# One weight row of wo split into sixteen uneven transfers, four one-row stores, and the small input loads on SyncE's queue

## The chip, the cores and the metric

The kernel runs on one core of one Trainium2 chip. The metric is device microseconds of one execution; the median of the three runs shown for the kernel before is 353.46 us (353.4, 353.46 and 354.35). One more execution was profiled; its own time was 353.3 us.

## The reference

A gated mix of two decode blocks for a single token. Cut to what matters:

```python
g = sigmoid((x * gate_w).sum(-1))            # one scalar
q = (x @ wq)                                  # 32 heads of 128
scores = q . k_cache * 128 ** -0.5            # 8 KV heads, 32768 keys, 4 q heads to each
o = softmax(scores) @ v_cache
a = o.reshape(1, 32 * 128) @ wo               # wo: 4096 x 512
b = (silu(x @ w_gate) * (x @ w_up)) @ w_down  # 512 -> 1792 -> 512
out = g * a + (1 - g) * b                     # 512 values, bf16
```

Everything is bf16. The K and V caches have 8 x 32768 x 128 values each, so nearly all that is read from memory is cache; wq and wo have 4 MB each, the three matrices of the second block 1.8 MB each.

## The kernel before, in words

The work is written as one instruction list for each engine, with semaphores between them; nothing is scheduled by a planner, so the order in the code is the order on the engine.

**SyncE (SP) issues all the large loads**, on one queue, in this order: wq (L297), w_gate and w_up (L299), then the K and V caches (L280). Each of the 8 groups (one KV head) has two K blocks and two V blocks of 4 MB. Four pages of on-chip memory hold them, so a load waits until the page's last reader is done: a K page until PE has transposed its last piece (`sem_fill`), a V page until PE has multiplied it (`sem_v_free`). Ahead of the last V block, SP issues the first piece of wo (`load_wo(0)`, L316); behind that V block come w_down (L322) and the other four pieces of wo. wo stands in memory as 128 partitions by 32 rows of 512 values; `WO_CUTS = [0, 8, 18, 26, 30, 32]` cuts the 32 rows into five pieces, each with a semaphore of its own (`sem_wo`).

**TensorE (PE)** first turns x and gate_w into columns (L338), multiplies with wq (L351), w_gate and w_up (L375), and then loops over the groups: transposes of K (L390), scores (L402), and the product with V (L446) of the group before. `emit_end` (L479) is the end of the program: the sum of the exponentials (L481), the last reduction (L428), w_down (L458), then the pieces of wo. Rows 0 to 17 (pieces 0 and 1) go through `emit_wide` (L458, one matmul for each row), rows 18 to 31 through `emit_rows` (L469, four matmuls for each row, one for each quarter of the output). Before each piece PE waits for that piece's semaphore (L501). After piece 2 the wide part is added (L513).

**VectorE (DVE)** copies transposed K to on-chip memory (L671) and at the end writes the result, `res_row` (L713): the four quarters of 128 values lie on partitions 0, 32, 64 and 96.

**ScalarE (ACT)** starts with two small loads, x and gate_w, one row of 512 values each (L527, L528), on its own queue. It computes the exponentials (L548). At the end SP stores the first two quarters of the result and ACT the other two (`store`, L204), each in one transfer of two rows. SP then waits for both (`sem_out` at 32, L329), and the program ends with the barrier of all engines (L210).

**GpSimd (POOL)** makes constants and takes the maximum over the partitions (L273); after the last of these, at about 319 us, it has nothing left but the closing barrier.

Of the kernel before, what the change touches and what calls it, by code (L numbers as in the profile page):

```python
# [13 lines left out]
def bass_gated_mix__gqa_block_cached__swiglu_ffn__decode_kernel(  # L14
# [41 lines left out]
    SCALE = float(DH) ** -0.5  # L56
    assert UPG == STEP == 4 * HPG and UPP % NKT == 0 and UPP % NST == 0
    assert KC * H * DH <= PAGE and 2 * KC * F <= PAGE and WOJ * NOUT <= PAGE
    WO_CUTS = [0, 8, 18, 26, 30, 32]
    WIDE = WO_CUTS[2]  # L60
    OC = NOUT // 128

    RQ = 4
# [10 lines left out]
    with ExitStack() as es:  # L74
        def S_(name):
            return es.enter_context(nc.semaphore(name))
# [3 lines left out]
        sem_f = S_("s_f")  # L80
        sem_wo = [S_(f"s_wo{i}") for i in range(len(WO_CUTS) - 1)]
        sem_ld_x = S_("s_ld_x")
# [5 lines left out]
        sem_out = S_("s_out")  # L88
# [39 lines left out]
        def T(name, shape, dt):  # L128
            return es.enter_context(nc.sbuf_tensor(name, shape, dt))

        x_row = T("x_row", [1, D], BF16)
        gw_row = T("gw_row", [1, D], BF16)
# [43 lines left out]
        res_row = T("res_row", [128, 128], BF16)  # L176
# [25 lines left out]
        wo_v = page[:, PG_X, 0 : WOJ * NOUT].rearrange("p (j n) -> p j n", j=WOJ)  # L202

        def store(eng, k):  # L204
            eng.dma_start(
                out[0, 0, 256 * k : 256 * (k + 1)].rearrange("(c n) -> c n", c=2),
                res_row[64 * k : 64 * k + 33 : 32, :],
            ).then_inc(sem_out, 16)

        with nc.Block("main") as block:  # L210
            @block.gpsimd
            def _(pool):
                pool.memset(ones_bf[:, :], 1.0).then_inc(sem_const, 1)
                pool.memset(ones_f[:, :], 1.0).then_inc(sem_const, 1)
                npool = [0]

                def chain(ins):
                    ins.then_inc(sem_pool, 1)
                    npool[0] += 1
                    pool.wait_ge(sem_pool, npool[0])  # L220

                chain(pool.memset(ident[:, :], 0.0))
                pool.affine_select(
                    out=ident[:, :],
                    in_=ident[:, :],
                    compare_op=ALU.not_equal,
                    fill=1.0,
                    base=0,
                    pattern=[[-1, 128]],
                    channel_multiplier=1,  # L230
                ).then_inc(sem_ident, 1)
                chain(pool.memset(ident_f[:, :], 0.0))
                pool.affine_select(
                    out=ident_f[:, :],
                    in_=ident_f[:, :],
                    compare_op=ALU.not_equal,
                    fill=1.0,
                    base=0,
                    pattern=[[-1, 128]],
                    channel_multiplier=1,  # L240
                ).then_inc(sem_ident, 1)
                chain(pool.memset(perm[:, :, :], 0.0))
                for e in range(2):
                    pool.affine_select(
                        out=perm[:, e, :],
                        in_=perm[:, e, :],
                        compare_op=ALU.not_equal,
                        fill=1.0,
                        base=-e,
                        pattern=[[0, 2], [-2, 64]],  # L250
                        channel_multiplier=1,
                    ).then_inc(sem_ident, 1)
                pool.iota(
                    colidx[:, :],
                    pattern=[[1, 128]],
                    base=0,
                    channel_multiplier=0,
                    allow_small_or_imprecise_dtypes=True,
                ).then_inc(sem_iota, 1)
                pool.iota(  # L260
                    kf[:, :],
                    pattern=[[1, 1]],
                    base=0,
                    channel_multiplier=1,
                    allow_small_or_imprecise_dtypes=True,
                ).then_inc(sem_iota, 1)
                pool.wait_ge(sem_dve_gpart, 1)
                pool.partition_all_reduce(gtot[:, :], gpart[:, :], 128, ReduceOp.add).then_inc(
                    sem_gtot, 1
                )  # L270
                for g in range(G):
                    pool.wait_ge(sem_pmax, STEP * (g + 1))
                    pool.partition_all_reduce(  # L273
                        gmax[:, g, :], pmax[:, g * STEP : g * STEP + HPG], 128, ReduceOp.max
                    ).then_inc(sem_gmax, 1)

            @block.sync
            def _(sp):
                def cache(which, g, b, p, sem):
                    sp.dma_start(  # L280
                        page[:, p, :].rearrange("p (r d) -> p r d", d=DH),
                        which[0, g, b * BLK : (b + 1) * BLK, :].rearrange("(p r) d -> p r d", r=R),
                    ).then_inc(sem, 16)

                def load_k(g, b):
                    if g:
                        sp.wait_ge(sem_fill, UPG * (g - 1) + UPP * (b + 1))
                    cache(A_k_cache, g, b, PG_K[b], sem_page[PG_K[b]])

                def load_v(g, b):  # L290
                    if g:
                        sp.wait_ge(sem_v_free, NB * (g - 1) + b + 1)
                    elif PG_V[b] == PG_F:
                        sp.wait_ge(sem_pe_h, 1)
                    cache(A_v_cache, g, b, PG_V[b], sem_page[PG_V[b]])

                sp.dma_start(wq_v, A_wq.rearrange("(p c) n -> p c n", c=KC)).then_inc(sem_q, 16)  # L297
                for w, src in enumerate((B_w_gate, B_w_up)):
                    sp.dma_start(  # L299
                        wgu[:, w, :, :], src.rearrange("(p c) f -> p c f", c=KC)  # L300
                    ).then_inc(sem_f, 16)
                for b in range(NB):
                    load_k(0, b)
                load_v(0, 0)
                load_k(1, 0)
                load_v(0, 1)
                load_k(1, 1)
                for g in range(2, G):
                    for b in range(NB):
                        load_k(g, b)  # L310
                        load_v(g - 1, b)

                def load_wo(k):
                    a, b = WO_CUTS[k], WO_CUTS[k + 1]
                    src = A_wo.rearrange("(p j) n -> p j n", j=WOJ)
                    sp.dma_start(wo_v[:, a:b, :], src[:, a:b, :]).then_inc(sem_wo[k], 16)  # L316

                load_v(G - 1, 0)
                sp.wait_ge(sem_pe_q, 1)
                load_wo(0)  # L320
                load_v(G - 1, 1)
                sp.dma_start(  # L322
                    wd[:, :, :], B_w_down.rearrange("(p j) n -> p j n", j=FC)
                ).then_inc(sem_ld_wd, 16)
                for k in range(1, len(sem_wo)):
                    load_wo(k)
                sp.wait_ge(sem_dve_row, 1)
                store(sp, 0)
                sp.wait_ge(sem_out, 32)  # L329

            @block.tensor
            def _(pe):
# [134 lines left out]
                def emit_rows(lhs, rhs, first, last):  # L467
                    for oc in range(OC):
                        ins = pe.matmul(  # L469
# [9 lines left out]
                def emit_end():  # L479
# [18 lines left out]
                    ).then_inc(sem_pe_O2, 1)  # L498
                    pe.wait_ge(sem_dve_O2, 1)
                    for k, s in enumerate(sem_wo):  # L500
                        pe.wait_ge(s, 16)  # L501
                        for j in range(WO_CUTS[k], WO_CUTS[k + 1]):
                            if j < WIDE:
                                ins = emit_wide(wo_v, O2, j, False, j >= WIDE - NSTRIP)
                            else:
                                ins = emit_rows(
                                    O2[:, j : j + 1], wo_v[:, j, :], j == WIDE, j == WOJ - 1
                                )
                        if k == 1:
                            ins.then_inc(sem_pe_w, 1)  # L510
                        if k == 2:
                            pe.wait_ge(sem_dve_w, 1)
                            emit_rows(sel4[:, 0:1], part[:, :], False, False)  # L513
# [10 lines left out]

            @block.scalar
            def _(act):
                act.dma_start(x_row[0:1, :], A_x[0, :, :]).then_inc(sem_ld_x, 16)  # L527
                act.dma_start(gw_row[0:1, :], gate_w.unsqueeze(0)).then_inc(sem_ld_x, 16)  # L528
                act.sem_inc(sem_exp, STEP)
                act.wait_ge(sem_gtot, 1)  # L530
                act.activation(g_col[:, :], gtot[:, :], ACT.Sigmoid).then_inc(sem_act_g, 1)
# [210 lines left out]
```

## Time and profile before

| what | value |
|---|---|
| time, median of three runs | 353.46 us |
| time of the profiled execution | 353.3 us |
| its span, first to last instruction | 351.5 us |
| PE busy | 263.6 us (75%) |
| DVE busy | 178.6 us (51%) |
| ACT busy | 32.1 us (9%) |
| read from memory | 148.11 MB, 421 GB/s over the span |
| last piece of wo in use | 348.54 us |
| result row written by DVE | from 348.97 us, 0.29 us |
| stores issued | 349.29 us |

The time of an execution holds about 1.8 us that lie outside the span. Busy shares are averages over stages with different limits, so they do not say what sets the time; that is read from the list of who waited for whom, and from the chain that ended last, which the profile follows back from the last instruction. The DMA rows count the packets of the 16 DMA engines; an issue row tells how long the issuing engine was held and how long after the issue the last byte had landed.

### The profile page before, as it was taken

What the parts mean: (1) busy time and instruction counts of PE and PEld (TensorE: products, weight loads), DVE (VectorE), ACT (ScalarE), POOL (GpSimd) and SP (SyncE); (2) the same over time, 40 slices, a digit from 0 to 9 for tenths busy, and PEclk for the clock granted to TensorE, in tenths of its full rate; (3) what the DMA queues carried; (4) which work ended last, traced back from release to release, by engine and by line L of the source; (5) the groups of instructions that cost most, each with busy time, mean ns of one, the idle gap of its engine ahead of it and who ended that gap; (6) DMA issues with size and microseconds to landing.
All of it is one profiled execution on the core that took longest, in us unless ns stands there. A gap on an engine that the chain in (4) does not pass through costs nothing.

```text
span 351.5 us, 8924 instructions
## 1 busy us (share of the span) xinstructions
PE 263.6 (75%) x4005; PEld 228.2 (65%) x4005; DVE 178.6 (51%) x204; ACT 32.1 (9%) x148; POOL 5.8 (2%) x24
## 2 busy tenths in 40 slices
PE   0446988898999959597797949794996749695464
PEld 0446978776796939395786839493966649593121
DVE  0311958565692938266563818283655628183011
ACT  1000000500120040002100040004000120004000
POOL 0200000000000000000000000000000000000000
PEclk9999969889996998769887978799889979898667
DMA  8999999999999999999999999999999999999995
GB/s 336 399 441 427 427 446 424 423 425 433 440 433 418 436 441 429 421 425 447 436 421 425 436 440 429 421 433 447 425 421 429 444 436 421 425 436 422 443 401 203
DMA packets 5924, 148.23 MB, mean 422 GB/s; under 512 B 666, under 2 KB 668, under 8 KB 924
## 3 DMA queue, kind: packets, MB, share of 16 engines
q1 hardware_dynamic: 5908, 148.11, 98.4%
q8 instruction: 6, 0.10, 0.1%
q14 instruction: 2, 0.02, 0.0%
q10 hardware_dynamic: 8, 0.00, 0.0%
HBM read 148.11 MB, written 0.00 MB: 421 GB/s over the span
## 4 chain that ended last, share of the span: by engine, by line
DMA 61%; PE 33%; DVE 3%; SPq 1%; issue 1%
DMA page<-in_A_k_cache_dram 54%; PE pst L390 24%; DMA page<-in_A_wo_dram 7%; PE ps_sc L402 6%; DVE ktT L671 3%; PE ps_o L446 2%; PE pst L469 1%; PE ps_m L428 0%; SPq L299 0%; SPq L316 0%; SPq L322 0%; SPq L297 0%; SPq L280 0%; DVE res_row L713 0%
## 5 line engine op out<-in xcount | busy, mean ns | idle before, releaser
L671 DVE COPY ktT<-pst 128x2048 bf16<-128x2048 bf16 x128 | 155.9, 1224 | 106.0 <-PE pst L390 98.9
L390 PE MATMUL pst<-ident_f,page 128*128 128x128 f32 x1024 | 156.6, 310 | 43.8 <-DMA page<-in_A_k_cache_dram 38.6
L390 PEld LDWEIGHTS pst<-ident_f,page 128*128 128x128 f32 x1024 | 133.1, 160 | 53.9 <-DMA page<-in_A_k_cache_dram 45.5
L402 PEld LDWEIGHTS ps_sc<-qcur,ktT 128*128 128x128 bf16 x2048 | 67.1, 97 | 11.4 <-DVE ktT L671 10.0
L402 PE MATMUL ps_sc<-qcur,ktT 128*128 128x8 bf16 x2048 | 67.9, 166 | 8.6 <-DVE ktT L671 8.6
L446 PE MATMUL ps_o<-page,ET 128*16 128x512 bf16 x512 | 40.5, 472 | 8.0 <-DMA page<-in_A_v_cache_dram 8.0
L446 PEld LDWEIGHTS ps_o<-page,ET 128*16 128x16 bf16 x512 | 13.1, 103 | 26.4 <-issue 19.2
L539 ACT ACTIVATE nbias<-gmax 128x4 f32<-128x4 f32 x8 | 1.6, 206 | 262.9 <-POOL gmax L273 262.9
L548 ACT ACTIVATE ET<-ps_sc,nbias 128x128 bf16<-128x128 f32 x64 | 23.9, 554 | 0.6
L548 ACT ACTIVATION_READ_ACCUMULATOR ET<-ps_sc,nbias 128x1 f32 x64 | 18.1, 283 | 0.0
L676 DVE TENSOR_REDUCE pmaxf<-ps_sc 128x4 f32<-128x512 f32 x16 | 11.1, 691 | 11.5 <-PE ps_sc L402 11.5
L428 PE MATMUL ps_m<-sel,acc 128*128 128x4 f32 x72 | 11.3, 280 | 3.9 <-ACT acc L560 3.9
L428 PEld LDWEIGHTS ps_m<-sel,acc 128*128 128x128 f32 x72 | 10.6, 226 | 4.5 <-ACT acc L560 4.5
L375 PE MATMUL ps_m<-xT,page 128*128 128x1 bf16 x112 | 6.9, 198 | 4.7 <-DMA page<-in_B_w_up_dram 4.7
L375 PEld LDWEIGHTS ps_m<-xT,page 128*128 128x128 bf16 x112 | 6.8, 162 | 4.9 <-DMA page<-in_B_w_up_dram 4.9
L694 DVE RECIPROCAL rS<-pst 128x32 f32<-128x32 f32 x1 | 0.4, 358 | 14.8 <-PE pst L481 14.8
L273 POOL PARTITION_ALL_REDUCE gmax<-pmax x8 | 3.0, 374 | 291.6 <-DVE pmax L678 291.6
L351 PE MATMUL ps_m<-xT,page 128*128 128x1 bf16 x128 | 3.6, 165 | 4.9 <-DMA page<-in_A_wq_dram 4.9
L560 ACT ACTIVATE acc<-ps_o 128x512 f32<-128x512 f32 x8 | 5.2, 652 | 16.7 <-PE ps_o L446 16.7
L351 PEld LDWEIGHTS ps_m<-xT,page 128*128 128x128 bf16 x128 | 3.5, 104 | 5.0 <-issue 5.0
L338 PE MATMUL ps_m<-ones_bf,x_row 1*128 1x1 bf16 x4 | 0.3, 172 | 8.5 <-DMA gw_row<-in_gate_w_dram 8.5
L338 PEld LDWEIGHTS ps_m<-ones_bf,x_row 1*128 1x128 bf16 x4 | 0.2, 114 | 8.5 <-DMA gw_row<-in_gate_w_dram 8.5
(68 smaller groups left out, 27.0 us busy)
## 6 DMA issues: line engine op xcount, KB each, us to landing
page<-in_A_k_cache_dram SPq DMA_DIRECT2D x16, 4096.0 KB, 27.2
page<-in_A_v_cache_dram SPq DMA_DIRECT2D x16, 4096.0 KB, 31.3
page<-in_A_wq_dram SPq DMA_DIRECT2D x1, 4096.0 KB, 13.0
page<-in_A_wo_dram SPq DMA_DIRECT2D x2, 1024.0 KB, 24.7
page<-in_B_w_gate_dram SPq DMA_DIRECT2D x1, 1792.0 KB, 16.9
page<-in_B_w_up_dram SPq DMA_DIRECT2D x1, 1792.0 KB, 21.2
wd<-in_B_w_down_dram SPq DMA_DIRECT2D x1, 1792.0 KB, 20.7
page<-in_A_wo_dram SPq DMA_DIRECT2D x1, 1280.0 KB, 23.3
```

The lines of the kernel that those rows point to most:

```text
L273: pool.partition_all_reduce(gmax[:, g, :], pmax[:, g * STEP : g * STEP + HPG], 128, ReduceOp.max).then_inc(sem_gmax, 1)
L351: ins = pe.matmul(ps_m[:, M_Q0 + h : M_Q0 + h + 1], wq_v[:, c, h * DH : (h + 1) * DH], xT[:, c : c + 1], start=(c == 0), stop=(c == KC - 1),)
L375: ins = pe.matmul(ps_m[:, base + j : base + j + 1], wgu[:, w, c, :].rearrange("d (p j) -> d j p", j=FC)[:, j, :], xT[:, c : c + 1], start= ...
L390: ins = pe.transpose(pst[u % NST][:, k * 128 : (k + 1) * 128], kv[:, n * 128 : (n + 1) * 128], ident_f[:, :],)
L402: ins = pe.matmul(ps_sc[b][:, col : col + 2 * HPG], kt[:, k, e, :], qcur[:, e, :], start=(e == 0), stop=(e == 1),)
L428: ins = pe.matmul(ps_m[:, M_P0 : M_P0 + HPG], acc[:, q, :], sel4[:, q * HPG : (q + 1) * HPG], start=(q == 0), stop=(q == RQ - 1),)
L446: ins = pe.matmul(ps_o[32 * c : 32 * c + RQ * HPG, :], ET[:, n : n + RQ, :].rearrange("p n h -> p (n h)"), view[:, k * RQ : (k + 1) * RQ, ...
L469: ins = pe.matmul(ps_c[32 * oc : 32 * oc + 1, 0:128], lhs, rhs[:, oc * 128 : (oc + 1) * 128], start=first, stop=last, skip_group_check=True,)
L548: act.activation(ET[:, b * R : (b + 1) * R, h], sc[:, h, :], ACT.Exp, bias=nbias[:, g, h : h + 1], scale=SCALE, accum_out=esum[:, g, b, h ...
L560: act.activation(acc[:, :, :].rearrange("p q d -> p (q d)"), ps_o[:, :], ACT.Copy).then_inc(sem_acc, STEP)
L671: dve.tensor_copy(ktT[:, u % NKT, :], pst[u % NST][:, :].bitcast(BF16)).then_inc(sem_cp, 1)
L676: dve.tensor_reduce(pmaxf[:, b, :], sc, AX.X, ALU.max).then_inc(sem_pmax, 4)
```

## The change

Four edits; no arithmetic changes.

1. The first piece of wo (rows 0 to 7) was one transfer. Now rows 0 to 6 are one transfer of 128 partitions, and row 7 is sixteen transfers of 15, 14, 13, 12, 11, 10, 9, 8, 8, 7, 6, 5, 4, 3, 2 and 1 partitions, 1 KB on each partition. All seventeen raise the same semaphore, for which PE waits at 272 instead of 16.
2. The last cut moves: piece 3 has five rows instead of four, piece 4 one row instead of two.
3. Each store of two rows becomes two stores of one row (SP two, ACT two). SP no longer waits for them; POOL does, at 64, after its last maximum.
4. The loads of x and gate_w move from ACT's queue to SP's, behind wq and ahead of w_gate.

```diff
-    WO_CUTS = [0, 8, 18, 26, 30, 32]
+    WO_CUTS = [0, 8, 18, 26, 31, 32]
+    STEPS = [15, 14, 13, 12, 11, 10, 9, 8, 8, 7, 6, 5, 4, 3, 2, 1]
+    assert sum(STEPS) == 128
...
         def store(eng, k):
-            eng.dma_start(
-                out[0, 0, 256 * k : 256 * (k + 1)].rearrange("(c n) -> c n", c=2),
-                res_row[64 * k : 64 * k + 33 : 32, :],
-            ).then_inc(sem_out, 16)
+            for c in (2 * k, 2 * k + 1):
+                eng.dma_start(
+                    out[0, :, 128 * c : 128 * (c + 1)], res_row[32 * c : 32 * c + 1, :]
+                ).then_inc(sem_out, 16)
...
                     ).then_inc(sem_gmax, 1)
+                pool.wait_ge(sem_out, 64)
...
                 sp.dma_start(wq_v, A_wq.rearrange("(p c) n -> p c n", c=KC)).then_inc(sem_q, 16)
+                sp.dma_start(x_row[0:1, :], A_x[0, :, :]).then_inc(sem_ld_x, 16)
+                sp.dma_start(gw_row[0:1, :], gate_w.unsqueeze(0)).then_inc(sem_ld_x, 16)
...
                 def load_wo(k):
                     a, b = WO_CUTS[k], WO_CUTS[k + 1]
                     src = A_wo.rearrange("(p j) n -> p j n", j=WOJ)
-                    sp.dma_start(wo_v[:, a:b, :], src[:, a:b, :]).then_inc(sem_wo[k], 16)
+                    if k:
+                        sp.dma_start(wo_v[:, a:b, :], src[:, a:b, :]).then_inc(sem_wo[k], 16)
+                        return
+                    sp.dma_start(wo_v[:, a : b - 1, :], src[:, a : b - 1, :]).then_inc(
+                        sem_wo[k], 16
+                    )
+                    p = 0
+                    for n in STEPS:
+                        sp.dma_start(
+                            wo_v[p : p + n, b - 1, :], src[p : p + n, b - 1, :]
+                        ).then_inc(sem_wo[k], 16)
+                        p += n
...
                 store(sp, 0)
-                sp.wait_ge(sem_out, 32)
...
-                        pe.wait_ge(s, 16)
+                        pe.wait_ge(s, 16 if k else 16 * (len(STEPS) + 1))
...
-                act.dma_start(x_row[0:1, :], A_x[0, :, :]).then_inc(sem_ld_x, 16)
-                act.dma_start(gw_row[0:1, :], gate_w.unsqueeze(0)).then_inc(sem_ld_x, 16)
                 act.sem_inc(sem_exp, STEP)
```

## The prediction

> **What bounds the kernel.** I read the DMA rows first, then the chain that ended last, then the rows of the last 12 us, then the issue rows of SP. On the page:
>
> ```profile
> DMA  8999999999999999999999999999999999999995
> q1 hardware_dynamic: 5908, 148.11, 98.4%
> HBM read 148.11 MB, written 0.00 MB: 421 GB/s over the span
> ```
>
> SP's queue (q1) keeps the 16 DMA engines busy for 98.4% of the span; only the first and last slice have a hole. So the time is the start, the stream of bytes, and what comes behind the last byte. A saving on PE, DVE or ACT inside the stream is worth nothing. The end of the chain, in order of time:
>
> ```profile
> 320.80 0.43 SPq L316
> 321.24 0.04 issue
> 321.28 25.32 DMA page<-in_A_wo_dram
> 346.59 0.04 issue
> 346.64 1.88 PE pst L469 x53
> 348.51 0.03 issue
> 348.54 0.41 PE pst L469 x8
> 348.95 0.02 issue
> 348.97 0.29 DVE res_row L713
> ```
>
> PE waits for wo, not wo for PE: the last piece arrives at 348.50, PE needs 0.41 us for it, DVE 0.29 us, and at 349.29 the stores go out. From there to the end of the span are 351.5 - 349.29 = 2.2 us, in which nothing computes. The change touches three things on this path: when the slowest DMA engine delivers the last piece, the 0.45 us of PE behind it, and the 2.2 us of stores and barrier.
>
> **1. The sixteen transfers.** Bytes are the same. The trace's packet records give one packet for one partition's run: 44 to 46 ns for 1 KB, 84 for 2 KB, 159 for 4 KB, 313 for 8 KB, and 9 ns for the increment that closes each engine's part of a transfer, with the next packet starting 6 ns after it. Row 7 was inside 8 KB packets, 8 of them on each engine. Taking it out makes each 8 KB packet one of 7 KB (about 274 ns) and one of 1 KB (45): 6 ns more, 8 x 6 = 0.05 us on each engine. What matters is where the sixteen transfers put their 128 packets. A one-partition load shows one data packet and a two-row store two, so I take n partitions as n engines. If each transfer starts at the same engine, the first engine gets 16 packets and 16 increments, the second 15, the eighth 9, the ninth 7, and the last none, where all had 8. The first engine then has 0.05 + 8 x 0.045 + 16 x 0.009 = 0.55 us more, the last 8 x 0.045 - 0.05 = 0.31 us less. [...]
>
> Does that move the end? PE waits for the latest engine. The sixteen increments of the last piece lie 1.86 us apart in the trace, with six engines in the first 0.4 us, two at 0.8 and 1.1, and eight between 1.45 and 1.86. This spread is there from about 130 us on and stays the same to the end, since all engines have equal work afterwards. Following the packets engine by engine, each of the eight late ones was held once or more by another queue (an instruction fetch of 16 KB takes 0.97 to 1.11 us, and the 32 KB packet beside it 1.7 instead of 1.21). If the late eight are the ones that are relieved, the end comes 0.31 us earlier at most; if the latest is the one that gets 16, it comes 0.55 us later. The engine that carried the packet of gate_w, the only one that can be named as the first, finishes 1.1 us behind the earliest and has 0.7 us to spare. But it began its first wq packet among the first eight engines, and the other seven of those are all among the late eight. If they are the low half, the late ones get 0.17 to 0.5 us more. This leans to a loss; I take **+0.2 us** (-0.31 to +0.55).
>
> Issue: seventeen SP instructions instead of one at 302.80. A wo transfer holds SP 0.43 us, a second one-row load 0.22 us (gw_row, below), the two-row store 0.60 us, with 0.04 us between. Sixteen more are 4.2 to 10.2 us, so SP is free by 313.4 at the latest:
>
> ```profile
> 302.43 0.33 SPq L280 DMA_DIRECT2D page<-in_A_v_cache_dram  x1
> 302.80 0.43 SPq L316 DMA_DIRECT2D page<-in_A_wo_dram  x1
> 319.96 0.33 SPq L280 DMA_DIRECT2D page<-in_A_v_cache_dram  x1
> ```
>
> The next thing queued on SP, the last V block, goes out at 319.96, when PE frees its page. The cover is 6.5 us, and the step costs **0**. PE reads piece 0 at 343.17 without waiting for it (it lands at about 327), so its later semaphore costs 0 too. [...]
>
> **2. The cut.** The last piece shrinks from 8 x 84 to 8 x 45 ns on each engine, so piece 3 lands 0.37 us ahead of the end instead of 0.65. PE starts piece 3 at 0.33 us before the last landing. In the rows of L469 a row of wo takes PE about 0.105 us, and the last of a run 0.31 us to its end. Five rows end their issue 0.53 us after the start, later than the last landing; the sixth then ends at -0.33 + 0.53 + 0.31 = 0.51 us behind the landing, against 0.45 now. **+0.05 us** (-0.1, if PE keeps up and only one row is left, to +0.15).
>
> **3. Stores and the end.**
>
> ```profile
> 0.72 0.53 ACTq L527 DMA_DIRECT2D x_row<-in_A_x_dram  x1
> 1.29 0.22 ACTq L528 DMA_DIRECT2D gw_row<-in_gate_w_dram  x1
> ...
> 349.29 0.60 SPq L205 DMA_DIRECT2D out_dram<-res_row  x1
> 349.30 0.58 ACTq L205 DMA_DIRECT2D out_dram<-res_row  x1
> ```
>
> No row shows two one-row stores in succession. Priced by the pair of one-row loads they hold the queue 1.29 + 0.22 - 0.72 = 0.79 us, 0.2 more than the one store; priced by the store row twice, 0.6 + 0.04 + 0.6 = 1.24, 0.65 more. From below: the data packet of x starts 0.98 us after its issue, that of the ACT store 1.5 us after; a second store 0.57 us behind, if it loses that half microsecond, gains nothing, and if only half the issue time is repeated, 0.25 us. Range -0.25 to +0.65; nearest are the loads, of the same shape and 1 KB: **+0.1 us**. For the wait: now SP sees the last increment, and POOL, which gathers the barrier, hears of it from SP's queue about 0.16 us later by the drain records. With POOL itself waiting that hop goes, unless POOL wakes later: **-0.1 us** (-0.2 to +0.2). Nothing is queued behind POOL's wait but the barrier.
>
> **4. x and gate_w on SP's queue.** They used to land at 8.5 us. Behind wq they land with it or up to 0.5 us later:
>
> ```profile
> 13.89 3.55 PE L351 MATMUL ps_m<-xT,page 128*128 128x1 bf16 x128 [4.92 <-DMA page<-in_A_wq_dram]
> 17.89 0.21 PE L362 MATMUL ps_o<-qT,perm 128*128 128x32 bf16 x2 [0.45 <-DVE qT L626]
> 22.85 1.31 PE L375 MATMUL ps_m<-xT,page 128*128 128x1 bf16 x19 [4.75 <-DMA page<-in_B_w_up_dram]
> ```
>
> PE's two groups of L338 and DVE's copies take 0.75 us before L351 can start, so L351 moves by at most 1.3 us, DVE's chain for the selection matrix with it. The cover is the 4.75 us that PE idles before L375, until w_up lands. **0**. Without the cover it would be 1.3 us. On SP two issues of 0.2 to 0.5 us stand ahead of w_gate, while wq's 4 MB keep the engines busy until 12 us: 0.
>
> **Sum.** 0.2 + 0.05 + 0.1 - 0.1 = +0.25 us on the profiled 353.3 us (span 351.5 and 1.8 outside): 353.55. That execution lies 0.16 us under the median of the runs shown, so I put the forecast at **353.7 us**. The bounds add up to -0.31 - 0.1 - 0.25 - 0.2 = -0.86 and 0.55 + 0.15 + 0.65 + 0.2 = +1.55, on the median 352.6 to 355.0.
>
> **Rivals.** (a) *Slower: SP's queue fills.* The most transfers seen outstanding on it without a stall is eight (the last V block of 302.43, piece 0 and the six issues from 319.96 on, at 322.6). After, some 19 are outstanding near 310. If the limit lies between, SP stands before its last small transfers until the V block of 302.43 has landed (324.5), issues the last V block too late, and the engines run dry for the 1.2 us from an issue to its first packet, or up to 5 us if eight small issues must come first. It decides from where SP is still in the small transfers after 325. 354.7 to 358.7, say 355.5. For it: nothing shows a depth over eight; against: no issue row is stretched at eight. Chance 0.08. (b) *Slower: the late engines get the load and each store costs its own 0.6 us.* Both upper bounds with the rest as above: 0.55 + 0.05 + 0.65 - 0.1 = +1.15, 354.6. For it: the seven early starters; against: the short second issue of gw_row. Chance 0.2. (c) *Faster: the ladder relieves the late engines*, and stores and barrier are at their lower bounds: 352.6. For it: a spread of 1.86 us to level; against: the first eight. Chance 0.17, less than half of it past 0.3%, as that takes a cause that I have not priced. (d) The forecast, terms cancel within half a microsecond: 0.55.
>
> A measurement of this kernel can tell about 0.3%, 1.06 us. Faster by that: 0.09 (part of c). Slower: 0.08 of (a), most of (b) and a little of (d), 0.29. Within: 0.62. The range is 352.6 to 355.0; it leaves out most of (a) and a bit on either side.
>
> **What would show it.** Right or wrong, step by step: the spread of the last piece's sixteen increments (1.86 now; over 2 means that the late engines got more); SP's L280 of the last V block still at PE's release near 320; L351 at most 1.3 us later and L375 unmoved; the time from the last landing to DVE's result row about 0.5 us; from the store's issue to the end of the span 2.0 to 2.9 us. The prediction fails if the DMA row shows a hole near 325, or if L375 or the first K block starts later.

## The result, and the profile after

The changed kernel takes 355.32 us (median of six runs, 354.91 to 355.73), the kernel before 353.89 us in runs beside it (353.40 to 354.44): a ratio of 1.0043, 95% interval 1.0032 to 1.0054, **1.5 us slower**. The forecast was 353.7, its range ended at 355.0. The profiled execution took 354.91 us, its span is 353.1 (before: 353.3 and 351.5). All further times are on the spans of profiled executions, or ratios with their intervals.

The page of the changed kernel, in the rows shown of before:

```profile
DMA  8999999999999999999999999999999999999994
q1 hardware_dynamic: 6168, 148.12, 98.3%
HBM read 148.11 MB, written 0.00 MB: 419 GB/s over the span
```

The engines are as busy as before (98.3% of the span; before 98.4%) with the same bytes: no hole. Busy is not fast, though. The end of the chain:

```profile
320.98 0.43 SPq L322
...
321.92 28.17 DMA page<-in_A_wo_dram
350.09 0.04 issue
350.13 0.59 PE pst L484 x24
350.72 0.02 issue
350.74 0.29 DVE res_row L726
```

The transfer at its head is now piece 3, 28.17 us from issue to landing; before it was piece 2, which takes 27.0 us now where it took 25.3. DVE writes the result row at 350.74 instead of 348.97. The last 24 matmuls now run in one go, as the last piece is there before PE has finished the one before it. By the landing records (the times at which a transfer's increments arrive) the last piece of wo lands at 350.42, before at 348.50: **1.93 us later**. From there to DVE's row PE needs 0.32 us instead of 0.47, and from that row to the end of the span are 2.38 us instead of 2.53. So the loss is 1.93 and everything behind it gives 0.3 back.

Where does the lateness come from? PE's wait for the last V block (before: 8.01 us, product from 336.81):

```profile
338.72 3.59 PE L461 MATMUL ps_o<-page,ET 128*16 128x512 bf16 x32 [10.88 <-DMA page<-in_A_v_cache_dram]
```

The V block that lies between the ladder (the sixteen transfers) and the end is already 1.9 us late. The last K block, ahead of the ladder, landed at nearly the same time in both (PE starts on it at 305.25; before 305.07). So the loss is made between, and the rate of the stream shows it. The view by windows gives, for 322 to 330 us, the busy times of the engines, the granted clock, the DMA share and last the GB/s. Before, and then the changed kernel:

```profile
322.00:330.00 8.00, 5.39 (x40) 2.75 (x40) 0.84 (x3) 1.37 (x7) 0.00 (x0) 0.57 1.05 446
```

```profile
322.00:330.00 8.00, 4.11 (x40) 1.96 (x40) 0.84 (x3) 1.52 (x9) 0.00 (x0) 0.71 1.03 381
```

In these 8 us 65 GB/s are missing, 0.52 MB, which at 446 GB/s are 1.2 us; the DMA share (1.03) looks full in both. The trace's packet records tell which packets stretched. The 1 KB packets themselves take 46 ns in the median, as priced. The first 32 KB packets of the V block behind them take 1.32 to 2.29 us; before, on all engines, 1.21 to 1.23.

### The profile page after: what moved, and what is told of

Its sections match the earlier page's. It is cut to its first block, busy times and chain, and to the rows that moved or that the text cites. A ratio compares the mean times of both kernels' runs of the same rounds, so it can differ in the third digit from the quotient of the medians.

```text
span 353.1 us, 8942 instructions
## 1 busy us (share of the span) xinstructions
PE 262.8 (74%) x4005; PEld 227.9 (65%) x4005; DVE 178.7 (51%) x204; ACT 32.3 (9%) x148; POOL 5.8 (2%) x24
## 3 DMA queue, kind: packets, MB, share of 16 engines
q1 hardware_dynamic: 6168, 148.12, 98.3%
## 4 chain that ended last, share of the span: by engine, by line
DMA 66%; PE 29%; DVE 2%; SPq 1%; issue 1%
DMA page<-in_A_k_cache_dram 58%; PE pst L405 22%; DMA page<-in_A_wo_dram 8%; PE ps_sc L417 5%; DVE ktT L684 2%; PE ps_o L461 1%; PE ps_m L443 0%; SPq L322 0%; SPq L304 0%; PE pst L484 0%; SPq L338 0%; SPq L300 0%; SPq L283 0%; SPq L301 0%; DVE res_row L726 0%
## 5 line engine op out<-in xcount | busy, mean ns | idle before, releaser
L405 PEld LDWEIGHTS pst<-ident_f,page 128*128 128x128 f32 x1024 | 134.8, 162 | 53.2 <-DMA page<-in_A_k_cache_dram 44.8
L443 PE MATMUL ps_m<-sel,acc 128*128 128x4 f32 x72 | 9.6, 257 | 3.8 <-ACT acc L573 3.8
L443 PEld LDWEIGHTS ps_m<-sel,acc 128*128 128x128 f32 x72 | 9.0, 196 | 4.4 <-ACT acc L573 4.4
L390 PE MATMUL ps_m<-xT,page 128*128 128x1 bf16 x112 | 6.9, 198 | 3.8 <-DMA page<-in_B_w_up_dram 3.8
L390 PEld LDWEIGHTS ps_m<-xT,page 128*128 128x128 bf16 x112 | 6.8, 158 | 3.9 <-DMA page<-in_B_w_up_dram 3.9
L366 PE MATMUL ps_m<-xT,page 128*128 128x1 bf16 x128 | 3.6, 165 | 0.3 <-DVE gwT L599 0.3
```

The costliest lines, as they stand in the source:

```text
L366: ins = pe.matmul(ps_m[:, M_Q0 + h : M_Q0 + h + 1], wq_v[:, c, h * DH : (h + 1) * DH], xT[:, c : c + 1], start=(c == 0), stop=(c == KC - 1),)
L390: ins = pe.matmul(ps_m[:, base + j : base + j + 1], wgu[:, w, c, :].rearrange("d (p j) -> d j p", j=FC)[:, j, :], xT[:, c : c + 1], start= ...
L405: ins = pe.transpose(pst[u % NST][:, k * 128 : (k + 1) * 128], kv[:, n * 128 : (n + 1) * 128], ident_f[:, :],)
L443: ins = pe.matmul(ps_m[:, M_P0 : M_P0 + HPG], acc[:, q, :], sel4[:, q * HPG : (q + 1) * HPG], start=(q == 0), stop=(q == RQ - 1),)
```

## The experiments

Three sets of theories follow one another. A and C: small packets, or only the uneven load. B (later B1 and I): the closing increments of transfers. B2: the number of transfers. P and M: neighbouring partitions in on-chip memory, or neighbouring rows in main memory (in the expectations, "look-ahead" for A and "ports" for P are the author's guesses at a cause, which no run shows). Microseconds are the ratio less one, times the median of before in the same set (353.6 to 354.0).

**First set: which edit, and what of it.** e1 is the changed kernel with the first piece in one transfer again; the others are the kernel before with only row 7 loaded otherwise, in this loop:

```diff
+                    p = 0
+                    for n in STEPS:            # e2: 15, 14, ..., 1; e3: [16] * 8; e4: [128]
+                        sp.dma_start(
+                            wo_v[p : p + n, b - 1, :], src[p : p + n, b - 1, :]
+                        ).then_inc(sem_wo[k], 16)
+                        p += n
```

> The changed kernel with row 7 of wo put back into the first piece's one transfer; the cut, the one-row stores, POOL's wait and x on SP's queue stay. If the sixteen transfers make the whole loss (in the changed kernel the last piece lands 1.93 us later, and the stretch behind it is 0.3 us shorter), this runs 0.2 to 0.4 us faster than the kernel before and its last V block's first packets take 1.21 to 1.23 us. Rival, stores or x on SP's queue make the loss: it stays 1 us or more slower than before.

> The kernel before with only the sixteen transfers of 15 down to 1 partitions. If they make the loss: 1.6 to 2.0 us slower than before, the sixteen increments of the last piece spread over more than 3 us instead of 1.86, and the first packet of the last V block takes 2.1 to 2.3 us instead of 1.22 on the engines that had many 1 KB packets. Rival (stores or x): within 0.4 us of before.

> The kernel before with row 7 loaded by eight transfers of 16 partitions: the same 128 packets of 1 KB, eight on every engine. Theory A, a run of 1 KB packets costs each engine the time of its look-ahead, so that the first large packet behind it takes some 0.9 us longer: 0.9 to 1.3 us slower than before, on all engines alike, spread of the last increments still about 1.9 us. Theory B, each closing increment of a transfer drains the engine: the same here, as there are eight. Theory C, only the uneven load counts: within 0.2 us of before.

> The kernel before with row 7 loaded by one transfer of its own over all 128 partitions: eight packets of 1 KB on every engine, one closing increment. Theory A (small packets): 0.7 to 1.3 us slower than before. Theory B (increments): within 0.2 us of before. Theory C (uneven load): within 0.2 us.

| run | ratio, interval | us |
|---|---|---|
| e1, all but the ladder | 0.9991 (0.9982 to 1.0000) | -0.3 |
| e2, ladder alone | 1.0039 (1.0026 to 1.0052) | +1.4 |
| e3, eight transfers of 16 | 1.0027 (1.0017 to 1.0036) | +1.0 |
| e4, one transfer of 128 | 1.0004 (0.9994 to 1.0014) | +0.1 |

The ladder makes the whole loss; stores, cut and the x loads together are no loss. The same 1 KB packets in one transfer cost nothing: theory A falls. Eight even transfers lose 1.0 us with a spread of 2.34 us between the first and the last increment of the last piece (before 1.86, e2 3.60): theory C alone falls too. What is left is what e3 has and e4 has not: seven more transfers, their increments, and sixteen neighbouring partitions in each.

**Second set: increments or transfers.** The same loop with more rows in each packet (e5: all eight rows, 8 KB; e6: rows 6 and 7, 2 KB), with `[32] * 4` (e7), and with `[8] * 16` (e8).

> The kernel before with the whole first piece (8 rows) loaded by eight transfers of 16 partitions: eight packets of 8 KB on each engine, each followed by a closing increment, so an increment every 0.32 us. Theory B1, a closing increment takes each engine some 0.12 us of write time that is only seen where less than that much data lies between two increments: within 0.2 us of before, and the last V block's first packets stay at 1.21 to 1.23 us. Theory B2, the number of transfers waiting on the queue is what costs: 0.8 to 1.1 us slower, as with eight transfers of 1 KB.

> The kernel before with rows 6 and 7 loaded by eight transfers of 16 partitions: eight packets of 2 KB on each engine, an increment every 0.09 us. Theory B1 (0.12 to 0.13 us for each increment with its data): 0.2 to 0.5 us slower. Theory B2 (number of transfers): 0.8 to 1.1 us slower, as with 1 KB.

> The kernel before with row 7 loaded by four transfers of 32 partitions: on each engine four times two 1 KB packets and one increment. Theory B1: four increments in 0.4 us are hidden by the data between them or nearly, 0 to 0.3 us slower. Theory B2: about half of eight transfers, 0.4 to 0.6 us.

> The kernel before with row 7 loaded by sixteen transfers of 8 partitions, each on eight engines: those eight get sixteen packets of 1 KB and sixteen increments, the other eight none. If the loss on an engine goes with its increments and the late engines are among these eight: 1.6 to 2.3 us slower, spread of the last increments over 3 us. If the late engines are the other eight: 0.2 to 1.0 us slower, spread under 2 us.

e5: 1.0158 (1.0143 to 1.0174), +5.6 us. e6: 1.0040 (1.0026 to 1.0054), +1.4. e7: 1.0015 (1.0006 to 1.0025), +0.5. e8: 1.0082 (1.0068 to 1.0096), +2.9. In e5 both theories failed: with 8 KB packets, increments lie 0.3 us and more apart and the number of transfers is that of e3, yet the loss grew more than fivefold. e6 lost more than either had; e7 what B2 had. Something in these transfers costs by the byte. In e5 the 8 KB packets take 0.62 us in the median (before 0.31). A transfer of 16 neighbours puts one partition on each engine (row 7 in sixteen transfers of together 128 partitions has 128 packets and 128 increments in the trace of the changed kernel), so all engines write into 16 neighbouring partitions, and read 16 neighbouring rows.

e8 lost more than the 1.6 to 2.3 us expected, but it answered its question. Eight engines have first V packets of 2.24 to 2.66 us, the other eight of 1.40 or less: here the sixteen transfers of eight went to the same eight engines. The first increment of the last piece comes 0.33 us later than before, the last 2.86 us later, spread 4.39 us: the latest engines are among the loaded ones.

**Third set: neighbours, where.** Eight transfers of 16 with 8 KB, spread on one side or both, and four of 32 in steps of four:

```diff
+                    for p in range(8):         # e10: only src in steps; e11: only wo_v in steps
+                        sp.dma_start(wo_v[p : 128 : 8, a:b, :], src[p : 128 : 8, a:b, :]
+                        ).then_inc(sem_wo[k], 16)
```

> As the eight transfers of 16 neighbouring partitions with 8 KB on each (+5.16 us), but each transfer takes every eighth partition, p, p + 8 and so on, of wo and of the page alike. Packets, increments, transfers and bytes are the same. [...] Theory B2, the number of transfers: 5 us slower again. [...]

> Reads every eighth row block of wo, but writes to sixteen neighbouring partitions (so the rows of wo stand on wrong partitions). Theory P (ports of on-chip memory): 4 to 6 us slower than before, as with neighbours on both sides. Theory M (main memory): 0 to 2.6 us slower.

> Reads sixteen neighbouring row blocks of wo, but writes to every eighth partition (so the rows of wo stand on wrong partitions). Theory P (ports of on-chip memory): 0 to 2.6 us slower than before. Theory M (main memory): 4 to 6 us slower.

> The first piece as four transfers of 32 partitions, every fourth one (p, p + 4 and so on), 8 KB on each: two packets and one increment for each engine and transfer. [...] Theory B2 (number of transfers): 2 to 3 us slower, half of what eight cost. [...]

| run | destination | source | ratio, interval | us | 8 KB packet, median us |
|---|---|---|---|---|---|
| e5 | neighbours | neighbours | 1.0158 (1.0143 to 1.0174) | +5.6 | 0.62 |
| e10 | neighbours | every 8th | 1.0142 (1.0108 to 1.0176) | +5.0 | 0.64 |
| e11 | every 8th | neighbours | 1.0112 (1.0085 to 1.0139) | +4.0 | 0.55 |
| e9 | every 8th | every 8th | 1.0120 (1.0103 to 1.0137) | +4.2 | 0.55 |
| e12 | every 4th | every 4th | 0.9998 (0.9989 to 1.0008) | -0.1 | 0.31 |

The packet times go with the destination and not with the source: theory M falls (e11's +4.0 us alone would have fitted it, e10's +5.0 does not). The bound of 2.6 us for every eighth partition was a miss; I had counted the piece alone, but the V blocks beside it stretch as well, in e9 by 1.1 us behind the piece and 0.7 ahead of it on the average engine. In e9 the longest 8 KB packet is 0.65 us, twice 0.31. In steps of four nothing is lost (e12, -0.1 us).

**Fourth set: hold the number of transfers.** e13 is one row in each transfer, eight of them, over all partitions; e14 is e12 with neighbours (`[32] * 4`, eight rows); e15 is the ladder over every eighth partition:

```diff
+                    for i, n in enumerate((15, 14, 13, 12, 11, 10, 9, 8)):
+                        for lo, hi in ((i, i + 8 * n), (i + 8 * n, 128)):
+                            sp.dma_start(wo_v[lo:hi:8, b - 1, :], src[lo:hi:8, b - 1, :]
+                            ).then_inc(sem_wo[k], 16)
```

> The first piece as eight transfers of one row each over all 128 partitions: eight transfers and eight increments on each engine as in the runs that lost 1 to 5 us, 64 packets of 1 KB on each. [...] Theory B2 (number of transfers): 1 to 5 us slower.

> The first piece as four transfers of 32 neighbouring partitions with 8 KB on each; with every fourth partition the same four transfers cost nothing (0.9998). Theory P: 1.5 to 5 us slower, packets of 8 KB stretched from 0.31 to 0.5 us or more. Theory B2: no slower than with every fourth partition, within 0.4 us.

> The kernel before with sixteen transfers of 15 down to 1 partitions of row 7 as in the change, each taking every eighth partition instead of neighbours: same sizes, packets, increments and, if a transfer's size sets its engines, the same load on each engine. [...] Theory C (uneven load alone makes it): 1.4 us slower as before.

e13: 1.0018 (1.0007 to 1.0029), +0.6, near the 0.4 us that 64 packets of 46 ns take over 8 of 313 (64 x 46 - 8 x 313 ns). B2 had 1 to 5 us for these eight transfers and 2 to 3 for the four of e12: it falls, clearly by e12 (-0.1), just outside the interval by e13. e14: 1.0128 (1.0112 to 1.0143), **+4.5**, against -0.1 for the same four transfers in steps of four; its 8 KB packets take 0.56 us in the median. PE's product with the last V block, e12 and then e14:

```profile
337.27 3.59 PE L452 MATMUL ps_o<-page,ET 128*16 128x512 bf16 x32 [7.28 <-DMA page<-in_A_v_cache_dram]
```

```profile
341.44 3.59 PE L454 MATMUL ps_o<-page,ET 128*16 128x512 bf16 x32 [11.35 <-DMA page<-in_A_v_cache_dram]
```

So neighbouring destination partitions cost by the byte; that is shown. (The source was spread in e12 too, but the third set shows that the source does not matter.) The 8 KB packets by the destination of a transfer: 0.31 us with every fourth partition (e12), 0.55 with every eighth (e9, e11), 0.56 with 32 neighbours (e14), 0.62 to 0.64 with 16 neighbours (e5, e10). Why it is so, no run shows.

But e15, 1.0051 (1.0037 to 1.0064), +1.8, went against P: the ladder spread over every eighth partition lost no less than the ladder of neighbours (e2, +1.4). That does not clear the destination, as every eighth partition had been nearly as dear as neighbours at 8 KB (e9 +4.2, e5 +5.6). Nor does it bring back theory C: its 1.4 us lies in the interval, but even transfers lose time too (e3). Back to the increments, in e17 and e18 with every fourth partition, as in e12.

**Fifth set: increments in a row.** e16 is e3 over every eighth partition, e17 is e7 in steps of four, e18 has sixteen transfers of 32 partitions in steps of four, half a row each:

```diff
+                    for j in (b - 2, b - 1):
+                        for lo in (0, 256):
+                            for p in range(4):
+                                sp.dma_start(wo_v[p : 128 : 4, j, lo : lo + 256],
+                                    src[p : 128 : 4, j, lo : lo + 256]).then_inc(sem_wo[k], 16)
```

> Row 7 by eight transfers of 16 partitions, every eighth one instead of neighbours (which lost 1.0 us). Theory I, closing increments in a row each hold the engine's writes some 0.17 us (their last landing came 1.7 us after the last packet with eight of them, 2.5 us with sixteen, 0.5 us with one): as before, 0.8 to 1.2 us slower, last landing again 1.5 us or more behind the last packet. Theory P (ports): at most 0.6 us slower.

> [...] Theory I: 4 x 0.17 less the 0.4 us that the packets take themselves, 0.2 to 0.5 us slower. Theory P: within 0.2 us of before, while the same with neighbours was 0.5 us slower.

> [...] Theory I: 16 x 0.17 less about 1 us of their own pace, 1.2 to 2.0 us slower, and the last V block's first packets stretched to 2 us or more on all engines. Theory P: within 0.5 us of before, first packets near 1.22 us.

e16 lost 1.3 us, about what theory I had, and its last landing came 1.85 us behind the last packet. e17 lost nothing (-0.2): here theory I, with 0.2 to 0.5 us, missed, and P was right. e18 lost 1.7 us, and the V block's first packets take 2.1 us or more on all engines: theory I was right, P wrong. e17 and then e18 by windows:

```profile
322.00:330.00 8.00, 4.23 (x40) 2.00 (x40) 0.84 (x3) 0.71 (x3) 0.00 (x0) 0.79 1.05 438
```

```profile
322.00:330.00 8.00, 4.12 (x40) 1.95 (x40) 0.84 (x3) 1.51 (x9) 0.00 (x0) 0.71 1.04 336
```

With four increments the stream keeps its rate (438 GB/s, before 446), with sixteen it loses a quarter (336), although the destination is every fourth partition in both. Put together from the landing and packet records ("lag" is from the end of the first piece's last packet to its last increment; "stretch" is what the V block's packets take over 1.216 us each, on the average engine):

| run | increments in a row on one engine | lag us | stretch us | ratio, interval |
|---|---|---|---|---|
| before | 1 | 0.46 | 0.02 | |
| e4 | 1 | 0.49 | 0.05 | 1.0004 (0.9994 to 1.0014) |
| e13 | 8, with 8 packets to each | 0.52 | 0.08 | 1.0018 (1.0007 to 1.0029) |
| e17 | 4, every 4th | 0.90 | 0.04 | 0.9995 (0.9986 to 1.0004) |
| e7 | 4, neighbours | 0.97 | 0.45 | 1.0015 (1.0006 to 1.0025) |
| e3 | 8, neighbours | 1.72 | 0.65 | 1.0027 (1.0017 to 1.0036) |
| e16 | 8, every 8th | 1.85 | 0.77 | 1.0038 (1.0025 to 1.0052) |
| e18 | 16, every 4th | 2.50 | 1.34 | 1.0048 (1.0034 to 1.0061) |
| e2, the ladder | 16 to 0 | 2.45 | 0.80 | 1.0039 (1.0026 to 1.0052) |
| e15, spread ladder | 16 to 0 | 2.48 | 0.84 | 1.0051 (1.0037 to 1.0064) |
| e8 | 16 on eight engines, 0 on eight | 2.50 | 0.93 | 1.0082 (1.0068 to 1.0096) |

The lag grows with the increments in a row and with nothing else in the table: 0.5, 0.9, 1.8, 2.5 us for 1, 4, 8 and 16, about 0.13 to 0.2 us for each, while the packets pass at 0.05 us each. The number of increments in all does not set it: for row 7 the engines of e2 and e8 make 128, as many as in e3 and half of e18's 256, and have the lag of e18. With four the next large packets are hardly stretched (e17, 0.04 us); with sixteen they are, by 1.34 us (e18). Eight were run only with neighbours and every eighth partition (e3, e16).

Theory I stands by e18, with two limits: its packets of 512 bytes were not run without the increments, and each increment closes a small transfer, so the two cannot be told apart. The destination works beside it. e7 against e17, the same four transfers, has a stretch of 0.45 against 0.04, and outside the table, in e5, e9 to e11 and e14, neighbours or every eighth partition alone bring the lag to 0.8 to 1.3 us with 8 KB packets between the increments (e12, every fourth: 0.46). The ladder writes to neighbours too, and no run has it on every fourth partition: how its stretch of 0.80 us divides between increments and destination is open.

## Why the prediction was wrong

**The failed step is the price of the sixteen transfers** in part 1: "the first engine then has 0.05 + 8 x 0.045 + 16 x 0.009 = 0.55 us more". What its engines do there is as priced: the 1 KB packets take 46 ns in the median, and the records of the increments still read 9 ns in the median (at most 18). What the sum put at nothing is what such a run does to the packets behind it: the 6 ns from the start of an increment to that of the next packet was read where one increment stands between two runs of large packets. It also put at nothing that a transfer to neighbouring partitions is slower by the byte (an 8 KB packet 0.56 us in e14, 0.31 in e12). Behind the ladder the first V packet of an engine takes up to 2.29 us instead of 1.22, and the second then about 1.47: 1.3 us that no row of before could show, and for which the bound of 0.55 left no room. On the average engine the last piece is 0.96 us late, and 0.80 us of that are the stretch of the V block's packets. The sum should have had an upper bound from a row further off.

**The direction inside the step was right.** The late engines do get the load: spread of the last piece 3.53 us instead of 1.86, and e8 names the loaded eight. By the landing records the last piece is 0.96 us later on the average engine and 1.93 on the latest (0.18 of it already there in the last K block, ahead of the ladder), so roughly half of the loss is common and half goes to the engines that were late already. The ladder levels in the wrong direction.

**SP's issue**: sixteen issues took 5.74 us, and the last V block went out at 320.11, as priced:

```profile
303.51 0.43 SPq L324 DMA_DIRECT2D page<-in_A_wo_dram  x1
303.99 5.74 SPq L329 DMA_DIRECT2D page<-in_A_wo_dram  x16
320.11 0.35 SPq L283 DMA_DIRECT2D page<-in_A_v_cache_dram  x1
...
320.98 2.82 SPq L322 DMA_DIRECT2D page<-in_A_wo_dram  x4
```

Rival (a)'s hold exists, but not where it would have cost time: the four last issues take 2.82 us instead of 1.86, with some twenty transfers outstanding. That 1 us is behind the V block, and those pieces wait in line for 20 us. The number of transfers does not make it: e8 has as many, and its four take 1.85 us. In e13 it stands ahead of the V block, with only ten transfers outstanding:

```profile
303.94 15.47 SPq L320 DMA_DIRECT2D page<-in_A_wo_dram  x8
321.71 0.33 SPq L280 DMA_DIRECT2D page<-in_A_v_cache_dram  x1
```

The last of these eight issues alone holds SP for 12.15 us. SP was free again at 319.41, before PE freed the page (321.71), so it cost nothing there either; in the kernel before, where the page comes free at 319.96, 0.55 us would have been left of the cover. What fills the queue is open.

**The cut** (+0.05): 0.32 us from the last landing to DVE's row, and 0.56 in e1, which has the same cut, against 0.47 before. Its sign stays open; the granted clock in these microseconds differs between the profiles (0.50 before at 348 to 349 us, 1.00 in the changed kernel at 350 to 351). **Stores and barrier** (0.0): from the issue to the last store's increment 1.62 us (e1 1.60) instead of 1.82, then 0.4 to 0.5 instead of 0.4: a gain of 0.1 to 0.2.

```profile
351.06 0.57 SPq L208 DMA_DIRECT2D out_dram<-res_row  x2
351.07 0.76 ACTq L208 DMA_DIRECT2D out_dram<-res_row  x2
```

Two one-row stores hold SP 0.57 us together, no more than the one of two rows (0.60). So rival (b) had the late engines right and the stores wrong. **x and gate_w** (0): right, with the cover that was named:

```profile
14.84 3.57 PE L366 MATMUL ps_m<-xT,page 128*128 128x1 bf16 x128 [0.32 <-DVE gwT L599]
...
22.88 6.88 PE L390 MATMUL ps_m<-xT,page 128*128 128x1 bf16 x112 [3.81 <-DMA page<-in_B_w_up_dram]
```

L366 starts 0.95 us later, L390 0.03 us later. The first K block, which I had named as a sign, starts 0.25 us later (32.90 instead of 32.65), but it lands as late in e4 (32.82 against 32.86), where x and gate_w load as before, so nothing can be read from that. The three edits without the ladder (e1) are the best version run: 0.9991 of the kernel before, with 1.0000 at the edge of the interval.

What stays open: why the packets behind increments in a row are stretched.

## What to carry to other kernels

In a stream that keeps all DMA engines busy, count closing increments: four in a row on each engine, with little data between, cost nothing into every fourth partition (e17, -0.2 us), sixteen stretched the packets behind them by 1.3 us (e18), and the loss was carried to the end (+1.7 us). A transfer into part of the partitions should spread its destination (four transfers for 1 MB: every fourth of 128 cost nothing, e12, -0.1 us; 32 neighbours 4.5 us, e14). And a price read where an operation stands alone is not the price of a run of them: for the increments it was too low, for the two stores in a row (0.57 us, not 0.60 each) too high.

## What the runs showed of the hardware

- The DMA share does not show either loss: 1.03 (changed kernel) and 1.04 (e18) of 16 engines at 322 to 330 us, while 381 and 336 GB/s pass instead of 446 (before, share 1.05). The stretched packets count as busy; the GB/s by window shows it.
- An increment's own record is short: 9 ns in the median, and the next packet starts 6 ns after its start. Sixteen in a row are not free for what stands behind them (e18: lag 2.50 us, next packets stretched by 1.34 us on the average engine).
- The engines' lateness towards each other stayed once made: the spread of a load's sixteen increments is 1.88 us at 138 us in the kernel before and 1.86 us in the last piece. In the changed kernel it is 2.19 us in the last K block, ahead of the ladder, and 3.5 us in the last V block and the last piece.
